# Four first-product blocks multiplied ahead of their Mish, and the seventh pair turned by DMA

## The chip, the core and the metric

The kernel runs on one core of a Trainium2 chip. The metric is the device time of one execution in microseconds, the median of several runs. The engines that appear below are PE (TensorE, matrix products and its transposes), DVE (VectorE), ACT (ScalarE), POOL (GpSimd) and SP (SyncE, which here only issues DMAs). PEld is PE's weight load. Each engine takes its own instructions in the order of the program; what has to wait, waits on semaphores.

## The reference

Attention with one extra term in the denominator, and behind it a two-layer block with Mish between the layers.

```python
# q, k, v: (8, 12, 448, 64); w_in: (768, 2048); w_out: (2048, 768)
scores = (1 / sqrt(64)) * q @ k.transpose(0, 1, 3, 2)
m = max(scores, axis=-1)
e = exp(scores - m)
attn = e / (sum(e) + exp(-m) + 1e-9)
x = (attn @ v), heads joined: (3584, 768)
h = x @ w_in                      # first product
g = h * tanh(log(1 + exp(h)))     # Mish
out = g @ w_out                   # second product
```

## The kernel before

**Pairs and units.** Two heads of one batch are a pair; a batch has six pairs, numbered through all batches (0 to 47). Three pairs are a unit, so a batch has two units. Pairs 0 to 5 (batch 0) run in a head of their own. After it comes a loop over units `u` from 2 to 17. A unit has two phases.

**Phase of the exponentials** (lines 586 to 619). It has 12 steps `n`, four for each pair. A step takes one or two score blocks of 128 rows x 448: `exps` issues the exponentials on ACT (L306), `flush_late` empties a queue of postponed copies out of PSUM onto DVE, `scores_ahead` issues the score products of the block three steps on (L272, L275, L266 and others) and their maximum on DVE (L293). There are three score tiles `sc0` to `sc2` in PSUM, of two banks each, used in turn, so the scores of step n + 3 wait for the exponentials of step n. In some steps there is other PE work: the product of a pair's weights with its values (`av_pair`, L382, whose copy into `xT` is L391), a transpose of a pair's weights on PE (`turn_on_pe`, L356, copied into `eT` by L360), and from unit 4 on pieces of the second product (L472, copied into `o_sb` by L459). In units 2 and 3 there are no such pieces.

**Phase of the first product** (lines 626 to 646). For `f` from 0 to 7 it runs `mm1_mish`: six products of 128x128 by 128x448 that make one of the 16 blocks `ff` of `h` of the batch before (L406), and Mish of it out of PSUM on ACT into `gT` (L412). Unit 2 makes the blocks 0 to 7 of batch 0, unit 3 the blocks 8 to 15. The block at f = 1 goes into a bank of `sc0`, the others take one of the two spare banks `mo`. Between the blocks stand the work for the pairs just done and for the next three: at f = 0 the denominators (L319, L323) and the division of the first pair's weights (`normalise`, seven L341 on DVE), at f = 3 that of the second pair, at f = 4 that of the third on POOL (seven L339, behind a small copy, L331); at f = 1, 3 and 5 the transposes of q and k of the next three pairs on PE (L193, into banks of `sc2` and `sc1`) and their copies out of PSUM (L214 and L227 on DVE, L235 on ACT); at f = 7 the scores of the first three steps of the next unit. At the end a one-element exponential (L649) brings ACT's table of exponentials back, since Mish has another.

**How weights are turned.** After the division a pair's weights `en` must be transposed into `eT` for `av_pair`. Most pairs go by a DMA transpose on SP's queue (L345). The pairs in `BY_PE` go by `turn_on_pe`, in four parts, at the steps listed in `TURN_AT`. `normalise` is called in an order that puts pairs of `BY_PE` last (`todo`). Pairs 6, 7 and 8 are unit 2's; 6 is the seventh pair, `HEAD` in the code. Before, 6 and 7 are both turned by PE in unit 3, and 8 by DMA.

**Other queues.** SP also issues the loads of q, k and v (L132), one pair four ahead at the steps 0, 3 and 6. POOL casts them to bf16 (L175, L176, L162) and issues the weight loads with a cast (L158, `load_w`) at the steps in `W_AT`. The blocks 8 to 11 of `h` read three pieces of `w_in` and the blocks 12 to 15 the next three. From pair 13 on, two pairs of three use a block-diagonal form of q in the tiles `q_diag`; their zero halves are written once, for pairs 13 and 14, by four DVE memsets in `evac_qk` (L223, L224), in unit 3's first-product phase.

**Banks.** `mo_take` gives the spare bank that has been free longest. In the phase of the exponentials a bank is free again when its postponed copy has run on DVE, one step later. `o_pool` has four tiles of 128 x 768 fp32, used for output rows, from unit 4 on.

Of the kernel before, what the change touches and what calls it, by code (L numbers as in the profile page):

```python
# [9 lines left out]
FP32 = mybir.dt.float32  # L10
# [9 lines left out]
def kernel(  # L20
# [91 lines left out]
    def flush_late():  # L112
        while late:
            late.popleft()()
# [86 lines left out]
    def evac_qk(p, act=False):  # L201
        if p >= N_PAIRS:
            return
        (q_ps, k_ps), own = qkT[p]
        mo_free.extend(own)
        qd = q_diag[p % 3]
        kT = qk_pool.tile([128, S], BF16, tag="kT", name="kT")
        if not is_diag(p):
            qT = qd.rearrange("d i h r -> d (i h r)")[:, 0:S]
            qkT[p] = (qT, kT)  # L210
            if act:
                nc.scalar.mul(qT, q_ps[:, 0:S], SCALE)
            else:
                nc.vector.tensor_scalar(  # L214
                    out=qT, in0=q_ps[:, 0:S], scalar1=SCALE, scalar2=None, op0=ALU.mult
                )
            if p >= DIAG_FROM:
                nc.gpsimd.tensor_copy(out=q_rest[0:64, 0, :], in_=qT[0:64, 384:S])
                nc.gpsimd.tensor_copy(out=q_rest[64:128, 1, :], in_=qT[64:128, 0:64])
        else:  # L220
            qkT[p] = (qd, kT)
            if p < DIAG_FROM + 3:
                nc.vector.memset(qd[0:64, :, 1, :], 0.0)  # L223
                nc.vector.memset(qd[64:128, :, 0, :], 0.0)  # L224
            for h in range(2):
                rows = slice(64 * h, 64 * h + 64)
                nc.vector.tensor_scalar(  # L227
                    out=qd[rows, :, h, :],
                    in0=q_ps[rows, 0:S].rearrange("d (i r) -> d i r", i=QB),
                    scalar1=SCALE, scalar2=None, op0=ALU.mult,  # L230
                )
        if p == 0 or own and not act:
            nc.vector.tensor_copy(out=kT, in_=k_ps[:, 0:S])
        else:
            nc.scalar.copy(kT, k_ps[:, 0:S])  # L235
# [160 lines left out]
        del att[p], casted[p], qkT[p]  # L396


    def mm1_mish(b, ff):
        if ff == 0:  # L400
            gT[b] = gT_pool.tile([128, FF_T, S], BF16, tag="gT", name="gT")
        flush_late()
        spare = ff % FF_U == 1
        h_ps = sc_tiles[0][:, 0, :] if spare else mo_take()
        for dm in range(DM_T):
            nc.tensor.matmul(  # L406
                h_ps[:, 0:S],
                lhsT=w_in_sb[:, dm, ff * 128 : (ff + 1) * 128],
                rhs=xT[b][:, dm, :],
                start=(dm == 0), stop=(dm == DM_T - 1),  # L410
            )
        nc.scalar.activation(out=gT[b][:, ff, :], in_=h_ps[:, 0:S], func=AF.Mish)  # L412
        if not spare:
            mo_free.append(h_ps)
# [78 lines left out]
    for g in range(B // 2):  # L493
# [12 lines left out]
        else:  # L506
# [8 lines left out]
    LAST_AV_AT = (0, 6, 9)  # L515
    HEAD = HP

    BY_PE = (2, 4, HEAD - 1, HEAD, HEAD + 1)
    TURN_AT = (
        {0: [(4, 2)], 1: [(4, 3)], **{3 + j: [(HEAD - 1, j)] for j in range(NT)}},  # L520
        {0: [(HEAD, 0), (HEAD, 1)], 1: [(HEAD, 2)], 2: [(HEAD, 3)],
         3: [(HEAD + 1, 0)], 4: [(HEAD + 1, 1)], 5: [(HEAD + 1, 2)], 6: [(HEAD + 1, 3)]},
    )
    TURN_HEAD = {
        (3, 2): [(2, 0)], (3, 3): [(2, 1)], (4, 0): [(2, 2)], (4, 1): [(2, 3)],
# [1 line left out]
    }  # L527
    AV_HEAD = {(3, 3): 0, (4, 2): 2, (4, 3): 1}
    W_HEAD = {0: 3, 1: 1, 3: 1, 4: 1}
    AV_AT = ({3: 4, 7: 3, 9: 5}, {5: 6, 8: 7, 10: 8})  # L530

    W_AT = ({5: 1, 9: 1}, {1: 1, 4: 1, 5: 1, 7: 1, 9: 1, 11: 1}, {3: 1, 5: 1, 7: 1, 9: 1})
    for which in ("qk", "v"):
# [41 lines left out]
    for u in range(UNITS_PER_B, N_UNITS + 2 * UNITS_PER_B):  # L575
# [10 lines left out]
        for n in range(steps):  # L586
# [22 lines left out]
            if u - UNITS_PER_B < len(AV_AT):  # L609
                early = AV_AT[u - UNITS_PER_B]  # L610
                if n in early:
                    av_pair(early[n])
                if u == UNITS_PER_B:
                    for part in TURN_AT[0].get(n, []):
                        turn_on_pe(*part)
            elif u == N_UNITS and n in LAST_AV_AT:
                av_pair(p0 - UNIT_PAIRS + LAST_AV_AT.index(n))
            if u - UNITS_PER_B < len(W_AT):
                load_w(W_AT[u - UNITS_PER_B].get(n, 0))
        assert done == total  # L620

        moe = u < N_UNITS + UNITS_PER_B
        b, w = (u - UNITS_PER_B) // UNITS_PER_B, u % UNITS_PER_B
        nxt = p0 + UNIT_PAIRS
        todo = sorted(range(p0, nxt), key=lambda p: p in BY_PE)
        for f in range(FF_U):
            if moe:
                mm1_mish(b, w * FF_U + f)
            if u == UNITS_PER_B and f in (2, 6):
                load_w(1)  # L630
            if not attn:
                continue
            if f == 0:
                denominators(att[p0]["whole"])
                normalise(todo[0], dma=todo[0] not in BY_PE)
            if f in (1, 3, 5):
                transpose_pair(nxt + f // 2, bank=f // 2 % 2)
                evac_qk(nxt + f // 2)
            if nxt < DIAG_FROM and f in (4, 6):
                scores_ahead(nxt * STEPS + f // 2 - 1)  # L640
            if f == FF_U - 1:
                scores_ahead(min(nxt * STEPS + 3, N_PAIRS * STEPS))
            if f == 3:
                normalise(todo[1], dma=todo[1] not in BY_PE)
            if f == 4:
                normalise(todo[2], dma=todo[2] not in BY_PE, on_pool=True)
# [37 lines left out]
```

## Time and profile before

| What | Value |
|---|---|
| median of 3 runs | 480.5 us (480.28 to 483.72) |
| profiled execution | 479.95 us |
| its span, first to last instruction | 478.0 us |
| mean granted TensorE clock | 0.982 |
| busy: PE, PEld, DVE, ACT, POOL | 443.1, 248.6, 339.1, 350.0, 181.1 us |
| mean of one L306 exponential, and of the accumulator read behind it | 637 and 206 ns |
| mean of one L293 maximum over two blocks | 968 ns |
| mean of one L406 product | 353 ns |

Times in what follows are microseconds from the span's start. A line of a timeline has start, duration, engine, line of the kernel, operation, output and input with their shapes, a count, and in brackets the idle time ahead and what ended it; merged instructions overlap in the pipe, so the distance from one start to the next (called the pitch below) is less than a duration. A line of stretches has the stretch, its length, the busy time of PE, PEld, DVE, ACT and POOL with counts, the granted clock as a share, the DMA share and the GB/s. In this execution unit 3's exponentials run from 76.75 to 91.9 and its first-product phase from there to 104.3.

### The profile page before, as it was taken

To read this page: it belongs to the slowest core of one execution; us is meant where nothing else is said; L and a number is where in the kernel's file an instruction comes from. 1 tells how busy PE (TensorE), PEld (TensorE's weight loads), DVE (VectorE), ACT (ScalarE), POOL (GpSimd) and SP (SyncE) were. 2 spreads that over 40 slices of the span, in tenths; PEclk is the share of its full clock that TensorE was granted. 3 is DMA by queue.
4 is the path that set the end of the run, shared out by engine and by line. 5 is a ranking of instruction groups with operands and counts; after the bars stand their busy time and mean duration, and the time that the engine had idled before them with its cause. 6 is when DMAs were issued, how large, how long until landed. Compare 5 with 4: busy or idle time off the path is not lost.

```text
span 478.0 us, 8924 instructions
## 1 busy us (share of the span) xinstructions
PE 443.1 (93%) x3064; PEld 248.6 (52%) x3064; DVE 339.1 (71%) x680; ACT 350.0 (73%) x919; POOL 181.1 (38%) x315
## 2 busy tenths in 40 slices
PE   4565888898999999999999999999999999999997
PEld 2233544454655555555555555556555555556565
DVE  4888987968787886878687878788787869420021
ACT  5979678878787888979787878888897978412300
POOL 4877809255514334353535242433535340300000
PEclk9998798899999999999999999999999999999999
DMA  8999969999999989899999999899989595870113
GB/s 228 220 233 220 235 100 234 162 187 238 207 217 276 206 212 219 213 203 246 193 250 182 225 167 228 211 207 234 201 233 212 156 178 127 135 164 24 43 28 105
DMA packets 202381, 90.37 MB, mean 189 GB/s; under 512 B 159072, under 2 KB 198880, under 8 KB 202336
## 3 DMA queue, kind: packets, MB, share of 16 engines
q1 hardware_dynamic: 194848, 83.51, 81.3%
q0 software_dynamic: 7488, 6.29, 8.6%
q8 instruction: 24, 0.39, 0.3%
q14 instruction: 21, 0.17, 0.1%
HBM read 45.61 MB, written 11.01 MB: 118 GB/s over the span
## 4 chain that ended last, share of the span: by engine, by line
PE 76%; ACT 10%; DVE 9%; issue 2%; DMA 1%; POOL 0%; SPq 0%; DVEq 0%; ACTq 0%; POOLq 0%
PE mo L472 26%; PE mo L406 25%; ACT en L306 9%; PE sc L382 6%; DVE negm L293 6%; PE sc L266 5%; PE sc L406 4%; PE sc L193 3%; PE sc L272 2%; PE mo L356 1%; PE mo L382 1%; DVE en L341 1%; PE sc L280 1%; DVE eT L360 1%; DMA k_f<-in_k_dram 1%
## 5 line engine op out<-in xcount | busy, mean ns | idle before, releaser
L306 ACT ACTIVATE en<-sc,negm 128x448 bf16<-128x448 f32 x336 | 209.6, 637 | 26.4 <-DVE xT L391 10.4
L293 DVE TENSOR_REDUCE negm<-sc 128x2 f32<-128x896 f32 x192 | 180.7, 968 | 55.8 <-PE sc L275 26.0
L472 PE MATMUL mo<-w_out_sb,gT 128*128 128x384 bf16 (+1 forms) x912 | 142.3, 301 | 0.0
L406 PE MATMUL mo<-xT,w_in_sb 128*128 128x448 bf16 x672 | 137.7, 353 | 0.6 <-DVE xT L391 0.6
L412 ACT ACTIVATE gT<-mo 128x448 bf16<-128x448 f32 x112 | 61.3, 547 | 68.2 <-PE mo L406 68.1
L472 PEld LDWEIGHTS <-gT 128*128 128x128 bf16 x912 | 84.1, 98 | 48.2 <-issue 5.7
L339 POOL TENSOR_SCALAR en<-en,rden 128x448 bf16<-128x448 bf16 x122 | 76.4, 646 | 80.7 <-DVE rden L331 76.9
L406 PEld LDWEIGHTS <-w_in_sb 128*128 128x128 bf16 x768 | 72.9, 98 | 64.0 <-issue 3.0
L306 ACT ACTIVATION_READ_ACCUMULATOR en<-sc,negm 128x1 f32 x336 | 69.3, 206 | 0.0
L175 POOL CAST q_bf<-q_f 112x512 bf16<-112x512 f32 x47 | 29.0, 617 | 98.4 <-DMA q_f<-in_q_dram 98.0
L341 DVE TENSOR_SCALAR en<-en,rden 128x448 bf16<-128x448 bf16 x214 | 58.6, 345 | 0.9
L459 DVE COPY o_sb<-mo 128x384 f32<-128x384 f32 (+1 forms) x65 | 32.2, 495 | 35.1 <-PE mo L472 34.8
L266 PE MATMUL sc<-kT,qd 128*128 128x448 bf16 x168 | 47.7, 354 | 0.3 <-ACT en L306 0.2
L272 PE MATMUL sc<-kT,qd 64*128 64x448 bf16 x72 | 25.1, 411 | 12.7 <-ACT en L306 11.1
L382 PE MATMUL sc<-eT,v_bf 112*64 112x448 bf16 x288 | 34.1, 357 | 1.9 <-ACT en L306 1.7
L162 POOL CAST v_bf<-v_f 112x512 bf16<-112x512 f32 x48 | 29.5, 616 | 9.7 <-DMA v_f<-in_v_dram 8.8
L382 PEld LDWEIGHTS <-v_bf 112*64 112x64 bf16 x384 | 21.0, 112 | 22.8 <-issue 13.6
L176 POOL CAST k_bf<-k_f 112x512 bf16<-112x512 f32 x47 | 28.9, 616 | 7.5 <-DMA k_f<-in_k_dram 7.0
L227 DVE TENSOR_SCALAR qd<-sc 64x448 bf16<-64x448 bf16 x48 | 18.7, 389 | 11.9 <-PE sc L193 11.2
L266 PEld LDWEIGHTS <-qd 128*128 128x128 bf16 x168 | 16.3, 97 | 18.0 <-issue 9.2
L275 PE MATMUL sc<-kT,qd 64*128 64x448 bf16 x72 | 25.4, 415 | 0.0
L472 PE MATMUL mo<-w_out_sb,mid 128*128 128x384 bf16 x128 | 24.9, 326 | 0.0
(57 smaller groups left out, 340.1 us busy)
## 6 DMA issues: line engine op xcount, KB each, us to landing
q_f<-in_q_dram SPq DMA_DIRECT2D x48, 224.0 KB, 5.1
k_f<-in_k_dram SPq DMA_DIRECT2D x48, 224.0 KB, 5.4
v_f<-in_v_dram SPq DMA_DIRECT2D x48, 224.0 KB, 5.7
w_in_sb<-in_moe_w_in_dram POOLq DMA_DIRECT2D x12, 256.0 KB, 6.1
w_out_sb<-in_moe_w_out_dram POOLq DMA_DIRECT2D x8, 384.0 KB, 7.6
out_dram<-o_sb SPq DMA_DIRECT2D x7, 336.0 KB, 3.3
out_dram<-o_sb SPq DMA_DIRECT2D x8, 288.0 KB, 4.6
out_dram<-o_sb SPq DMA_DIRECT2D x8, 240.0 KB, 2.9
```

Of the source, the lines that this page charges most:

```text
L162: nc.gpsimd.tensor_copy(out=casted[p][2], in_=loaded.pop(p)[2])
L266: nc.tensor.matmul(sc[:, bk, 0:S], lhsT=qT[:, i].rearrange("d h r -> d (h r)"), rhs=kT, start=True, stop=True,)
L272: nc.tensor.matmul(sc[:, 0, 0:S], lhsT=qT[0:64, qa : qa + 128], rhs=kA, start=True, stop=True)
L293: nc.vector.tensor_reduce(out=negm, in_=sc[:, 0 : len(cols), 0:S], axis=AX.X, op=ALU.max, negate=True)
L306: nc.scalar.activation(out=st["en"][:, :, c, 0:SP_], in_=sc[:, bk, 0:S].rearrange("q (j c) -> q j c", j=NT), func=AF.Exp, bias=st["negm"][ ...
L339: nc.gpsimd.tensor_scalar(scalar2=1.0, op0=ALU.mult, op1=ALU.mult, **args)
L341: nc.vector.tensor_scalar(scalar2=None, op0=ALU.mult, **args)
L382: nc.tensor.matmul(av[h * 64 : (h + 1) * 64, 0:S], lhsT=v_bf[:, h, j * D : (j + 1) * D], rhs=e_h, start=(j == 0), stop=(j == NT - 1),)
L406: nc.tensor.matmul(h_ps[:, 0:S], lhsT=w_in_sb[:, dm, ff * 128 : (ff + 1) * 128], rhs=xT[b][:, dm, :], start=(dm == 0), stop=(dm == DM_T - 1),)
L412: nc.scalar.activation(out=gT[b][:, ff, :], in_=h_ps[:, 0:S], func=AF.Mish)
L459: nc.vector.tensor_copy(out=o_sb[:, cols], in_=st["o"][:, 0:n_cols])
L472: nc.tensor.matmul(st["o"][:, 0:n_cols], lhsT=src[:, ff, c0 : c0 + 128], rhs=w_out_sb[:, ff, cols], start=(ff == 0), stop=(ff == FF_T - 1),)
```

## The change

- In unit 3's phase of exponentials, at the steps 5, 7, 9 and 10, `mm1_ahead` issues the products of the blocks 8, 9, 10 and 11 of batch 0 into an `mo` bank, and queues a DVE copy into an fp32 tile of `o_pool` (128 x 448 used), which runs at the next step.
- In unit 3's first-product phase the order of the blocks is 8, 12, 9, 13, 10, 14, 11, 15. The blocks 8 to 11 have only their Mish there, read from the fp32 tile. The bank of `sc0` goes to the block at f = 1, which is now 12.
- Pair 6 leaves `BY_PE`: it is turned by DMA. So `todo` in unit 2 is 6, 8, 7 in place of 8, 6, 7: pair 6 is divided and sent at f = 0, pair 8 at f = 3.
- Pair 7 is turned by PE at the steps 1 to 4 of unit 3 (before 3 to 6; pair 6 was at 0 to 2). The value products of pairs 6, 7 and 8 stand at the steps 3, 6 and 8 (before 5, 8 and 10).
- The zero halves of `q_diag[1]` and `q_diag[2]` are written by four POOL memsets at the end of unit 3's exponentials.

```diff
             qkT[p] = (qd, kT)
-            if p < DIAG_FROM + 3:
-                nc.vector.memset(qd[0:64, :, 1, :], 0.0)
-                nc.vector.memset(qd[64:128, :, 0, :], 0.0)
...
-    def mm1_mish(b, ff):
-        if ff == 0:
-            gT[b] = gT_pool.tile([128, FF_T, S], BF16, tag="gT", name="gT")
-        flush_late()
-        spare = ff % FF_U == 1
-        h_ps = sc_tiles[0][:, 0, :] if spare else mo_take()
+    def mm1(b, ff, h_ps):
         for dm in range(DM_T):
...
+    h_sbs = {}
+
+    def mm1_ahead(b, ff):
+
+        h_ps = mo_take()
+        mm1(b, ff, h_ps)
+        h_sb = o_pool.tile([128, d_model], FP32, tag="o_sb", name="o_sb")
+        h_sbs[b, ff] = h_sb
+
+        def evac():
+            nc.vector.tensor_copy(out=h_sb[:, 0:S], in_=h_ps[:, 0:S])
+            mo_free.append(h_ps)
+
+        late.append(evac)
+
+    def mm1_mish(b, ff, spare):
+        if ff == 0:
+            gT[b] = gT_pool.tile([128, FF_T, S], BF16, tag="gT", name="gT")
+        flush_late()
+        if (b, ff) in h_sbs:
+            nc.scalar.activation(out=gT[b][:, ff, :], in_=h_sbs.pop((b, ff))[:, 0:S], func=AF.Mish)
+            return
+        h_ps = sc_tiles[0][:, 0, :] if spare else mo_take()
+        mm1(b, ff, h_ps)
         nc.scalar.activation(out=gT[b][:, ff, :], in_=h_ps[:, 0:S], func=AF.Mish)
...
-    BY_PE = (2, 4, HEAD - 1, HEAD, HEAD + 1)
+    BY_PE = (2, 4, HEAD - 1, HEAD + 1)
     TURN_AT = (
         {0: [(4, 2)], 1: [(4, 3)], **{3 + j: [(HEAD - 1, j)] for j in range(NT)}},
-        {0: [(HEAD, 0), (HEAD, 1)], 1: [(HEAD, 2)], 2: [(HEAD, 3)],
-         3: [(HEAD + 1, 0)], 4: [(HEAD + 1, 1)], 5: [(HEAD + 1, 2)], 6: [(HEAD + 1, 3)]},
+        {1 + j: [(HEAD + 1, j)] for j in range(NT)},
     )
...
-    AV_AT = ({3: 4, 7: 3, 9: 5}, {5: 6, 8: 7, 10: 8})
+    AV_AT = ({3: 4, 7: 3, 9: 5}, {3: 6, 6: 7, 8: 8})
+    FIRST_AT = {5: FF_U, 7: FF_U + 1, 9: FF_U + 2, 10: FF_U + 3}
+    SECOND = [ff for i in range(4) for ff in (FF_U + i, FF_U + 4 + i)]
...
                 if n in early:
                     av_pair(early[n])
+                if u == UNITS_PER_B + 1 and n in FIRST_AT:
+                    mm1_ahead(0, FIRST_AT[n])
...
+        if u == UNITS_PER_B + 1:
+            for t_ in q_diag[1:]:
+                nc.gpsimd.memset(t_[0:64, :, 1, :], 0.0)
+                nc.gpsimd.memset(t_[64:128, :, 0, :], 0.0)
+
...
             if moe:
-                mm1_mish(b, w * FF_U + f)
+                mm1_mish(b, SECOND[f] if u == UNITS_PER_B + 1 else w * FF_U + f, spare=f == 1)
```

## The prediction

> **What bounds the kernel now.** I began with the page's chain of waits, to see which engine sets the end.
>
> ```profile
> PE 76%; ACT 10%; DVE 9%; issue 2%; DMA 1%; POOL 0%; SPq 0%; DVEq 0%; ACTq 0%; POOLq 0%
> ```
>
> Three quarters of the chain are PE, so PE work that is taken off a stretch where PE is the limit, and put where PE idles, is worth its length. The change lies in unit 3, so next came the busy time by stretch: unit 3's exponentials, its first-product phase, then the same two of unit 4.
>
> ```profile
> 76.75:91.90 15.15, 11.62 (x86) 6.71 (x86) 12.97 (x19) 13.44 (x43) 9.94 (x16) 0.79 1.16 208
> 91.90:104.30 12.40, 12.40 (x87) 6.75 (x86) 8.98 (x29) 8.60 (x18) 4.65 (x9) 0.98 0.90 160
> 104.30:119.30 15.00, 13.07 (x89) 7.22 (x88) 12.76 (x18) 13.56 (x44) 7.83 (x14) 1.00 1.08 228
> 119.30:130.10 10.80, 10.80 (x87) 6.48 (x86) 7.63 (x24) 8.18 (x16) 5.00 (x10) 1.00 1.31 205
> ```
>
> In unit 3's first-product phase PE is busy for all of 12.40 us, DVE and ACT for under 9. In the exponentials PE leaves 3.5 us, and runs at a mean clock of 0.79. The chain in order of time shows PE's part:
>
> ```profile
> 88.64 2.84 PE mo L382 x16
> 91.48 1.67 PE mo L406 x6
> 93.16 1.13 PE sc L406 x6
> ...
> 100.02 2.29 PE mo L406 x12
> ...
> 102.89 1.28 ACT L649
> ```
>
> Two value products and the first block ran at a low clock (one value product is 0.95 at full clock, one block 1.13). Then ACT and DVE in the same place, and ACT's pitch in unit 4's phase:
>
> ```profile
> 92.17 1.28 ACT L412 ACT_TABLE_LOAD   x1
> ...
> 121.18 0.54 ACT L412 ACTIVATE gT<-sc 128x448 bf16<-128x448 f32 x1
> 121.60 0.54 ACT L235 COPY kT<-sc 128x448 bf16<-128x448 bf16 x1
> 122.01 0.57 ACT L412 ACTIVATE gT<-mo 128x448 bf16<-128x448 f32 x1
> ```
> ```profile
> 87.74 2.61 DVE L293 TENSOR_REDUCE negm<-sc 128x2 f32<-128x896 f32 x3
> 90.26 0.61 DVE L391 CAST xT<-mo 128x448 bf16<-128x448 f32 x1
> 91.52 0.62 DVE L391 CAST xT<-mo 128x448 bf16<-128x448 f32 x1 [0.65 <-PE mo L382]
> 92.18 0.18 DVE L319 SCALAR_TENSOR_TENSOR den<-sums,expm 128x21 f32<-128x21 f32 x1
> 92.40 0.29 DVE L323 RECIPROCAL rden<-den 128x21 f32<-128x21 f32 x1
> 92.73 1.81 DVE L341 TENSOR_SCALAR en<-en,rden 128x448 bf16<-128x448 bf16 x7
> ```
>
> ACT issues a Mish or copy each 0.42 us when nothing holds it, and DVE begins the division as soon as its last copy is done. Last SP's queue, the landing of its transposes between 60 and 160, and the first consumer in unit 4:
>
> ```profile
> 67.42 4.20 SPq L345 DMA_TRANSPOSE eT<-en  x1
> 71.72 0.53 SPq L132 DMA_DIRECT2D q_f<-in_q_dram  x1
> ...
> 95.03 13.69 SPq L345 DMA_TRANSPOSE eT<-en  x3
> ```
> ```profile
> DMA to landing us min/median/max: 6.1/6.6/9.3
> ```
> ```profile
> 105.67 0.95 PE L382 MATMUL sc<-eT,v_bf 112*64 112x448 bf16 x8 [0.32 <-ACT en L306]
> ```
>
> **Unit 2: the transposes.** Pair 6 goes at 67.42 in pair 8's place; it lands by 75 to 77 and is read at step 3, near 82.5. Pair 8 follows at 71.7 and lands by 81 at the latest; it is read near 88.5. Behind it on SP the nine loads of pairs 13 to 15 start 4.2 us later, at 75.9. They land 4.2 to 7.0 us after issue in this stretch, so POOL's casts of pairs 13 and 14 slip by 2 to 3 us, and so does the weight load queued behind the first of them (at 81.33 before), of the last piece that block 12 needs. With 6.1 to 7.7 us to landing it is there by 90 to 92; block 12 is due at 92.5 (below). q and k of these pairs are due from 94. All covered, by a margin under 2 us for the weight piece; if that is gone, PE waits for what is missing.
>
> **Unit 3: the exponentials.** PE loses four turns at 0.55 and gains four blocks at 1.13: 2.3 us more, against 3.5 idle. DVE loses four L360 copies and gains four fp32 copies, 128x448. L391, the same input shape, has a pitch of 0.53, and so has L360: no change in sum, only in place. Up to the maximum of step 8 (ends 86.67) as many copies lie ahead as before. From there: copy of block 8 (0.53), maximum of step 9 (1.0), L391 of pair 7 (0.53), maximum of 10 (1.0), copy of block 9 (0.53), maximum of 11 (0.53). Step 9's maximum is ready at 88.2 (before 88.74), step 11's at 90.8. ACT starts step 9 at 88.3, step 10 at 89.8, and ends at 91.85 with L316, 0.3 earlier than before. The moved blocks stand ahead of the next scores on PE; with 1.13 + 0.3 a step on PE and 1.53 on DVE, DVE still sets the step.
>
> The last block is the tight one. Its bank is that of pair 8's value product, whose copy stands behind the maximum of step 11: 90.8 + 0.53 = 91.3. So block 11 runs from 91.35 to 92.5, and its copy, which DVE must take before the denominators, ends at 93.05. L319 then starts 0.87 later than the 92.18 shown.
>
> **Unit 3: the first-product phase, engine by engine.** PE: block 12 to 93.65, then 3 transposes of 0.4 and blocks 13 to 15, ended at 98.3 with its waits; before 102.3. ACT: table 1.28 to 93.15, eleven instructions of about 0.43 with waits for blocks 13, 14 and 15 (1.0 in all), to 98.8, table and L649 (1.4): exponentials at 100.3. Mish from fp32 in SBUF is in no row. Bounds: 0.54, as from PSUM, and 0.617, a cast of 112x512 from SBUF on ACT in the head; 4 x 0.07 = 0.3 at most, inside the waits. I take 0.54, the nearer shape. DVE: from 93.05, in the pitches of before, denominators 0.55, seven L341 1.80, L214 0.37, two L227 0.82, seven L341 1.73, L331 0.15, two L227 0.80: 99.3. The four memsets (0.24 each, 1.3 with their gaps) are gone; on POOL they fall between its last weight issue and 93, where it sits idle for 8 us. First maximum 1.03: 100.3. So ACT and DVE meet at 100.35, against 104.29: **3.95 us gained.**
>
> **Unit 4.** Pair 9's division ends at 95.4; SP took 0.57 to start and 6.2 to land: 102.1. Its value product came 1.38 behind the first exponential, so would now be due at 101.7: 0.4 lost, on the way to the scores and maximum of step 3, which DVE and ACT then wait for. The next two transposes follow SP's own pace (4.3 each): landed at 106.4 and 110.8, due at 107.5 and 112.4. SP's loads start at 108.8, as before, while what reads them is due 3.5 us earlier: pair 17's casts end near 118, its transposes are due at 121.8; the last second-product weights land 8.2 us after 118.3 to 119, due from 127.5. All hold, by 1 to 4 us. Behind unit 4 nothing is changed, and units repeat at PE's pace, so the shift lasts. **Net 3.95 - 0.4 = 3.55 us.** The profiled execution of 479.95 (span 478.0 and 1.95 around it) becomes 476.4; it lay 0.55 under the median of the runs, which becomes 477.0.
>
> **Rivals.**
> - *No late division.* If the bank waits overlap better, ACT is the floor: 93.15 + 11 x 0.42 + 1.4 = 99.2, or 5 us gained, and the median 475.5. For it: all waits are sums of pitches that I made by hand. Against: DVE's order, which is fixed. 0.16.
> - *Given back in unit 4.* The transpose of pair 9 takes the 9.3 seen at the longest, not 6.2: 3.1 lost, 480.0. For it: that row, and that SP and its loads don't move with the rest. Against: 9.3 belongs to the stretch with a DMA share of 1.31, and here it was 0.57 from 92 to 96. 0.12.
> - *Half clock (slower).* These are single microseconds of before, with the clock third from the end:
>
> ```profile
> 79.00:80.00 1.00, 0.88 (x7) 0.39 (x6) 0.86 (x2) 1.00 (x5) 1.00 (x2) 0.50 0.96 252
> 87.00:88.00 1.00, 0.00 (x0) 0.00 (x0) 1.00 (x3) 1.00 (x3) 0.00 (x0) 1.00 1.32 196
> 90.00:91.00 1.00, 1.00 (x8) 0.37 (x4) 0.88 (x2) 1.00 (x5) 0.00 (x0) 0.50 1.33 206
> ```
>
>   The clock is 0.50 from 79 to 82 and 89 to 92, each time behind a gap on PE. If it stays at 0.50 from 82 to the end of the exponentials, four blocks cost 2.26 each (+4.5), two value products 2.84 (+0.95), four scores +0.2 each: 6.3 us, nearly all on PE's path to block 11, since PE has 7.8 us of work in the 8.1 from 84.4. Then 477.0 + 6.3 = 483.3; with blocks 12 and 13 as well, 485.6. It ends slower than before once more than 3.55 of the 6.3 comes, over half of the stretch. For it: in the head the clock stayed at 0.50 from about 44.5 to 54.8, with PE busy nine tenths from 46 on. Against: steps 1 to 3 are as before, so the clock should rise at 82 again, and the gap at 87 is filled by a block. 0.10.
>
> The Trainium skill, page "TensorE: Matmul & The Clock Gate", section "Part 1: The HAM clock gate", has half clock after an idle window of about 3.4 us and full clock after as long a busy one; by it the fuller stretch stays at full clock and this rival falls away. The trace agrees on the length of the low stretches here, but a gap of only 1.4 us (86.9 to 88.3) was enough to bring one, and the head's low stretch lasted three times as long, so I leave the rival its chance.
>
> **The numbers.** My forecast, 3.55 us with about a microsecond of hand-summed waits either way (2.2 to 4.6 gained, 475.9 to 478.3), has 0.62. Within 1% (475.7 to 485.3) is what a measurement of this kernel can't tell from no change. Faster beyond that: the first rival, 0.16. Slower beyond: the half clock that lasts into the next phase or a missing weight piece, 0.07. Within: 0.77. The range reaches from 475.2, past the ACT floor, to 481.0, past the transpose that takes 9.3; about 0.2 is left out, mostly the half clock.
>
> **What would show it.** Right: exponentials of unit 4 near 100.3, L319 of unit 3 near 93, block 11 ended past 92, a clock of 1.0 from 82 on, pair 9's value product waiting some tenths for its DMA, and all of unit 5 3.5 us earlier. Wrong: maxima of unit 3 late behind blocks at 2 us each; block 12 waiting for its weights; a wait of over 1 us at a value product of unit 4; POOL's casts of pairs 16 and 17 holding unit 4's transposes.

## The result and the profile after

| | before | after |
|---|---|---|
| median of 20 runs each, us | 480.14 (478.97 to 483.72) | 483.63 (481.1 to 486.95) |
| ratio after / before, with its 95% interval | | 1.0062 [1.0045, 1.0079] |
| profiled execution, us | 479.95 | 484.43 |
| its span, us | 478.0 | 482.4 |
| mean granted TensorE clock | 0.982 | 0.985 |

The changed kernel is 0.6% slower, 3.5 us by the medians, where I had forecast 3.5 us less. The ratios leave out the runs in a slower state (one of e6 below, two of e10, three of e12), and the medians take in all runs.

Line numbers below are those of the changed kernel where its trace is read: exponentials L303, maximum L290, denominators L316 and L320, division L338, DMA transpose L342, value product L379, first product L398, copy into SBUF L415, Mish from SBUF L425 and from PSUM L429, second product L489, table of exponentials L674.

The shares of the chain of waits by engine, after:

```profile
PE 70%; ACT 12%; DVE 9%; DMA 5%; issue 3%; POOL 1%; SPq 0%; DVEq 0%; ACTq 0%
```

DMA has grown from 1% to 5% of the chain, 19 us or so longer in it, and PE has given up 6%. Almost all of that is two transposes that unit 5 waits for (10.69 and 7.69). The chain only runs through them: 19 us more of it don't cost 19 us, but waits for transfers are where to look. To place the loss I used ACT's table loads as marks, since each phase begins with one. After, on ACT's timeline:

```profile
68.67 1.28 ACT L429 ACT_TABLE_LOAD   x1
...
95.60 1.28 ACT L425 ACT_TABLE_LOAD   x1
...
103.59 1.28 ACT L674 ACT_TABLE_LOAD   x1
...
121.24 1.28 ACT L429 ACT_TABLE_LOAD   x1
...
131.88 1.28 ACT L674 ACT_TABLE_LOAD   x1
...
149.93 1.28 ACT L429 ACT_TABLE_LOAD   x1
```

The same marks before stand at 64.99, 92.17, 102.89, 119.44, 128.76 and 145.53. The first belongs to unit 2, ahead of anything that the change touches, and is already 3.68 late. Taken off, the rest reads as a shift, negative where the changed kernel is ahead: **-0.25** at the end of unit 3's exponentials, **-2.98** at the end of its first-product phase, **-1.88** and **-0.56** at the same two places of unit 4, **+0.72** at the end of unit 5's exponentials. From unit 6 on both kernels keep the same pace but for one step of 0.10 us, and 0.72 is what is left at the end of the span. So the trace holds three stories: the head (3.68), a gain of 2.98 up to the end of unit 3, and 3.70 given back in the units 4 and 5.

The stretches of the changed kernel between these marks (a phase of exponentials is counted from 1.40 behind its L674 mark, where the first exponential can start), first unit 3's two phases, then unit 4's, then unit 5's exponentials:

```profile
80.41:95.60 15.19, 12.97 (x91) 6.67 (x91) 12.83 (x19) 13.89 (x45) 11.36 (x19) 0.89 1.11 236
95.60:104.99 9.39, 8.50 (x65) 4.69 (x64) 8.24 (x26) 8.26 (x14) 2.98 (x8) 1.00 1.31 172
104.99:121.24 16.25, 13.65 (x93) 7.49 (x91) 12.81 (x18) 13.68 (x45) 7.05 (x12) 1.00 1.10 237
121.24:133.28 12.04, 10.88 (x87) 6.49 (x86) 9.52 (x24) 8.21 (x14) 8.44 (x15) 1.00 1.27 203
133.28:149.93 16.65, 15.41 (x99) 8.09 (x97) 12.54 (x18) 13.85 (x45) 3.72 (x7) 1.00 1.07 234
```

Unit 3's first-product phase went from 12.12 (92.17 to 104.29) to 9.39, and PE is no longer busy throughout. Unit 4's two phases took 16.25 and 12.04, against 15.15 and 10.73 before, and unit 5's exponentials 16.65 against 15.36, with the same work in them. DVE's busy time in unit 4's first-product phase rose from 7.70 to 9.52 for the same 24 instructions.

**Where it is given back.** Three places. The first is the value product of pair 9 in unit 4, on PE's timeline after:

```profile
107.46 0.95 PE L379 MATMUL sc<-eT,v_bf 112*64 112x448 bf16 x8 [0.96 <-DMA eT<-en]
```

Its transpose was issued at 99.49 and took 7.8 us to land. The second is the division of pair 12 at the start of unit 4's first-product phase, DVE before and then DVE after:

```profile
120.00 1.81 DVE L341 TENSOR_SCALAR en<-en,rden 128x448 bf16<-128x448 bf16 x7
```
```profile
121.86 3.58 DVE L338 TENSOR_SCALAR en<-en,rden 128x448 bf16<-128x448 bf16 x7
```

The same seven instructions take twice as long. POOL's timeline shows what runs beside them after, and where the same casts of pair 17 stood before:

```profile
121.85 0.64 POOL L175 CAST q_bf<-q_f 112x512 bf16<-112x512 f32 x1
122.40 0.70 POOL L176 CAST k_bf<-k_f 112x512 bf16<-112x512 f32 x1
123.06 0.60 POOL L162 CAST v_bf<-v_f 112x512 bf16<-112x512 f32 x1
123.61 1.49 POOL L158 DMA_DIRECT2D w_out_sb<-in_moe_w_out_dram  x2
```
```profile
116.62 0.63 POOL L175 CAST q_bf<-q_f 112x512 bf16<-112x512 f32 x1
117.18 0.63 POOL L176 CAST k_bf<-k_f 112x512 bf16<-112x512 f32 x1
117.74 0.62 POOL L162 CAST v_bf<-v_f 112x512 bf16<-112x512 f32 x1
```

Before, the casts were done ahead of the division. Now, counted from the head, DVE arrives 1.8 us earlier (121.86 less 3.68, against 120.00) and POOL 1.6 later (121.85 less 3.68, against 116.62). The third place is the chain in order of time, which follows the late division into unit 5:

```profile
122.56 2.88 DVE en L338 x6
125.44 0.06 DVE qd L214
125.50 10.69 DMA eT<-en
```

The transpose of pair 12 is issued at 125.50, beside the weight loads just shown, lands after 10.69 us, and the value product of unit 5 waits for it. PE's timeline there, after and before:

```profile
125.79 0.36 PE L193 MATMUL sc<-ident,q_bf 112*128 112x112 bf16 x4 [1.16 <-DVE qd L214]
...
131.89 3.44 PE L489 MATMUL mo<-w_out_sb,gT 128*128 128x192 bf16 x28
136.33 0.95 PE L379 MATMUL sc<-eT,v_bf 112*64 112x448 bf16 x8 [1.00 <-DMA eT<-en]
```
```profile
128.77 3.44 PE L472 MATMUL mo<-w_out_sb,gT 128*128 128x192 bf16 x28
132.15 0.95 PE L382 MATMUL sc<-eT,v_bf 112*64 112x448 bf16 x8
```

Before, that product ran without a gap. But its transpose, issued at 121.87, had taken 9.3 us, by its line's transposes from 121 to 123 in the trace before:

```profile
DMA to landing us min/median/max: 9.3/9.3/9.3
```

It landed at 131.2, 1.0 us ahead of its use. In this pair of traces, that margin is what was used up.

### The profile page after: what moved, and what is told of

It reads as the page before. It is cut to its first block, busy times and chain, and to the rows that moved or that the text cites. A ratio compares the mean times of both kernels' runs of the same rounds, so it can differ in the third digit from the quotient of the medians.

```text
span 482.4 us, 8867 instructions
## 1 busy us (share of the span) xinstructions
PE 440.6 (91%) x3036; PEld 245.9 (51%) x3036; DVE 345.1 (72%) x676; ACT 350.0 (73%) x919; POOL 182.5 (38%) x319
## 4 chain that ended last, share of the span: by engine, by line
PE 70%; ACT 12%; DVE 9%; DMA 5%; issue 3%; POOL 1%; SPq 0%; DVEq 0%; ACTq 0%
PE mo L489 25%; PE mo L398 23%; ACT en L303 9%; PE sc L379 6%; PE sc L263 5%; DVE negm L290 5%; DMA eT<-en 4%; PE sc L193 3%; PE sc L398 3%; PE sc L269 2%; DVE en L338 2%; PE mo L379 1%; DMA w_in_sb<-in_moe_w_in_dram 1%; PE mo L353 1%; DMA k_f<-in_k_dram 1%
## 5 line engine op out<-in xcount | busy, mean ns | idle before, releaser
L303 ACT ACTIVATE en<-sc,negm 128x448 bf16<-128x448 f32 x336 | 209.2, 636 | 32.0 <-DVE negm L290 14.9
L290 DVE TENSOR_REDUCE negm<-sc 128x2 f32<-128x896 f32 x192 | 180.7, 969 | 57.2 <-PE sc L272 24.8
L489 PE MATMUL mo<-w_out_sb,gT 128*128 128x384 bf16 (+1 forms) x912 | 142.3, 301 | 0.0
L398 PE MATMUL mo<-xT,w_in_sb 128*128 128x448 bf16 x672 | 137.6, 352 | 1.3 <-DMA w_in_sb<-in_moe_w_in_dram 0.6
L489 PEld LDWEIGHTS <-gT 128*128 128x128 bf16 x912 | 84.1, 98 | 48.0 <-issue 5.5
L429 ACT ACTIVATE gT<-mo 128x448 bf16<-128x448 f32 x108 | 59.1, 547 | 65.1 <-PE mo L398 64.7
L398 PEld LDWEIGHTS <-w_in_sb 128*128 128x128 bf16 x768 | 72.8, 98 | 64.0 <-issue 3.2
L303 ACT ACTIVATION_READ_ACCUMULATOR en<-sc,negm 128x1 f32 x336 | 69.1, 206 | 0.0
L338 DVE TENSOR_SCALAR en<-en,rden 128x448 bf16<-128x448 bf16 x214 | 65.1, 375 | 0.9
L379 PE MATMUL sc<-eT,v_bf 112*64 112x448 bf16 x288 | 34.1, 357 | 3.8 <-DMA eT<-en 2.2
L269 PE MATMUL sc<-kT,qd 64*128 64x448 bf16 x72 | 25.5, 411 | 12.8 <-ACT en L303 11.1
L379 PEld LDWEIGHTS <-v_bf 112*64 112x64 bf16 x384 | 20.3, 110 | 24.1 <-issue 13.3
L489 PE MATMUL mo<-w_out_sb,mid 128*128 128x384 bf16 x128 | 24.9, 326 | 0.0
```

The source lines that it names most:

```text
L269: nc.tensor.matmul(sc[:, 0, 0:S], lhsT=qT[0:64, qa : qa + 128], rhs=kA, start=True, stop=True)
L290: nc.vector.tensor_reduce(out=negm, in_=sc[:, 0 : len(cols), 0:S], axis=AX.X, op=ALU.max, negate=True)
L303: nc.scalar.activation(out=st["en"][:, :, c, 0:SP_], in_=sc[:, bk, 0:S].rearrange("q (j c) -> q j c", j=NT), func=AF.Exp, bias=st["negm"][ ...
L338: nc.vector.tensor_scalar(scalar2=None, op0=ALU.mult, **args)
L379: nc.tensor.matmul(av[h * 64 : (h + 1) * 64, 0:S], lhsT=v_bf[:, h, j * D : (j + 1) * D], rhs=e_h, start=(j == 0), stop=(j == NT - 1),)
L398: nc.tensor.matmul(h_ps[:, 0:S], lhsT=w_in_sb[:, dm, ff * 128 : (ff + 1) * 128], rhs=xT[b][:, dm, :], start=(dm == 0), stop=(dm == DM_T - 1),)
```

## The experiments

In all of them the shift is counted as above, from the first mark. The table gives each run's median, its ratio to the kernel before measured beside it, and the shift of its profiled execution at the ends of unit 3, unit 4 and unit 5, each time behind the unit's first-product phase.

| run | median, us | ratio [95%] | unit 3 | unit 4 | unit 5 |
|---|---|---|---|---|---|
| after, first trace | 483.63 | 1.0062 [1.0045, 1.0079] | -2.98 | -0.56 | +0.61 |
| e1_after_again | 483.35 | 1.0055 [1.0036, 1.0073] | -2.79 | -1.26 | +1.38 |
| e2_after_spread | 484.97 | 1.0095 [1.0065, 1.0124] | -1.89 | -0.11 | +1.28 |
| e3_before_spread | 482.98 | 1.0050 [1.0026, 1.0073] | -1.13 | -1.13 | -1.31 |
| e4_turn_only | 483.78 | 1.0080 [1.0053, 1.0108] | -0.79 | +0.05 | +1.13 |
| e5_before_again | 480.57 | 1.0007 [0.9987, 1.0027] | -0.90 | -0.90 | +0.21 |
| e6_blocks_only | 483.96 | 1.0075 [1.0052, 1.0099] | -1.44 | +0.11 | +2.44 |
| e7_turn_only | 482.60 | 1.0046 [1.0021, 1.0070] | -2.09 | -0.41 | +1.18 |
| e8_loads_first | 481.80 | 1.0025 [1.0002, 1.0049] | -2.97 | +0.97 | +0.23 |
| e9_weights_early | 481.59 | 1.0015 [0.9993, 1.0037] | -2.19 | +2.97 | +2.23 |
| e10_after_both | 489.09 | 1.0198 [1.0151, 1.0244] | -2.17 | +3.40 | +2.66 |
| e11_before_both | 483.61 | 1.0065 [1.0040, 1.0090] | -0.90 | +1.76 | +1.02 |
| e12_turn_both | 492.84 | 1.0185 [1.0137, 1.0232] | +3.41 | +6.07 | +5.33 |
| e13_split | 484.80 | 1.0085 [1.0048, 1.0123] | -2.98 | +2.26 | +1.53 |
| e14_after_half | 478.88 | 0.9963 [0.9937, 0.9990] | -2.71 | -2.45 | -3.19 |
| e15_loads_half | 478.20 | 0.9944 [0.9922, 0.9965] | -2.19 | -1.83 | -2.56 |
| e16_before_half | 479.28 | 0.9976 [0.9955, 0.9997] | -1.12 | -1.11 | -1.85 |
| e17_gated | 478.00 | 0.9954 [0.9939, 0.9968] | -2.98 | -2.45 | -3.19 |
| e18_behind | 478.11 | 0.9957 [0.9941, 0.9973] | -2.64 | -2.26 | -3.00 |

### Is the head's 3.68 us the change's?

The head's instructions are the same in both kernels. Yet in the first trace after, three early divisions on DVE took 5.20 us where before they took 0.82. DVE's timeline after, then before:

```profile
17.40 5.20 DVE L338 TENSOR_SCALAR en<-en,rden 128x448 bf16<-128x448 bf16 x3
```
```profile
17.36 0.82 DVE L341 TENSOR_SCALAR en<-en,rden 128x448 bf16<-128x448 bf16 x3
```

POOL was at work without a gap beside the long ones: it issued three weight loads, divided four blocks and cast until 22.46. In none of the other traces did the three take over 1.50. e1 is the changed kernel unaltered.

> The changed kernel, unaltered. In its first profile the head alone, whose program is the same on every engine as before, came out 3.7 us longer: three divisions on DVE (L338, at 17.4) lasted 5.2 us in place of 0.8 while POOL went from issuing weight loads straight into its own divisions and casts. Theory A (chance of an execution, set by when the first loads land): the times fall into two groups about 3.5 us apart, near 481.5 and 484.5, and a profile shows either 5.2 or 0.8. Theory B (the change lengthens the head every time): one group near 484, and 5.2 in the profile.

Its first mark stands at 65.56, so most of the 3.68 was this one execution; but its units 4 and 5 gave back 4.2 us again. Of the three places, the first is missing: pair 9's transpose landed after 7.0, and PE did not wait for it. The other two are there: the division of pair 12 took 3.48, its transpose 12.0, and the value product of unit 5 waited 2.32. e2, e3 and e4 spread the weight loads of the head, on the kernel after, the kernel before, and the kernel before with pair 6 turned by DMA:

```diff
-    W_HEAD = {0: 3, 1: 1, 3: 1, 4: 1}
+    W_HEAD = {0: 1, 1: 1, 2: 1, 3: 1, 4: 1, 5: 1}
```

> The changed kernel with the head's first three weight loads issued one per pair instead of three at once, so that POOL is done with them before DVE's first divisions at 17.4. Theory A: the three divisions take 0.8 to 1.2, unit 2's first Mish table load begins near 65 as before the change, and the time is one group near 481 (480.1 plus the 0.7 that the units 3 to 5 lost net in the profile). Theory B: still near 484.

> The kernel before with the same spreading of the head's weight loads. Theory A: the same 480 as before, since it met the stretch of 5.2 in few runs; e2 minus e3 is then what units 3 to 5 do, 0.7 to 1.5 us lost. If spreading itself costs or brings something, it shows here.

> Of the change only pair 6 turned by DMA, with the later order of pairs and value products, on the kernel before with spread weight loads; no block is multiplied ahead. Theory C (SP's queue gives the gain back: the second transpose in unit 2 pushes nine loads and two weight loads 4 us later, and they then run beside unit 3's transposes): pair 9's transpose lands later than the 6.2 of before, POOL's casts of pair 13 wait for their loads, and the time is 0.5 to 3 us above e3. Theory D (what was lost in units 4 and 5 comes from their being due earlier, not from the extra transpose): same as e3 within 0.5, or faster by the DVE copies saved.

A miss: spreading costs by itself. e3 is 0.5% over the kernel before, its first mark at 68.83, e2's at 68.62 and e4's at 67.47. So against the kernel before the medians of these three tell nothing on the change. Against e3, which has the same spreading, e2 is 2.0 us longer and e4 0.8, with intervals that overlap. Their shifts show unit 4 and 5 losing 3.2 us in e2 and 1.9 in e4, and nothing in e3. e5 is the kernel before, unaltered.

> The kernel before, unaltered, sent like an experiment: a second profile of it and a second set of times. If the head's length is a matter of chance for each execution of this program, its times lie on the 480.2 of the runs of before, and the head ends (unit 2's first Mish table load) within 0.5 of 65.0 in the profile. If sending a kernel as an experiment alone adds time, it comes out near 483 like the last four.

The first mark lies at 66.83 this time, and the median did not move. Over the three traces that run before's program up to this mark (64.99, e5 66.83, e16 65.64) it has a mean of 65.8; in e1, which has the change, it is 65.56. The head varies from one execution to the next, and no run ties that to the change.

e5 shows a second thing. On its PE timeline, at the end of unit 3's exponentials, stand the value products and the first block that the chain of before has at 88.64 and 91.48 with 2.84 and 1.67 us:

```profile
90.44 1.70 PE L382 MATMUL mo<-eT,v_bf 112*64 112x448 bf16 x16
92.80 1.30 PE L406 MATMUL mo<-xT,w_in_sb 128*128 128x448 bf16 x6 [0.66 <-DVE xT L391]
```

The low clock of this place in the trace that I predicted from did not come again. e5 is 0.90 ahead of that trace behind unit 3, and e3, e11 and e16 are 0.9 to 1.1 ahead as well. So the first trace was about 1.0 us worse up to the end of unit 3 than the other four of the kernel before and its variants, and of the gain of 2.98 about 2.0 is the change's.

e5 shows a third thing. The kernel before can lose in unit 5 too. There pair 12's transpose took 10.4, and PE's timeline has

```profile
133.34 0.95 PE L382 MATMUL sc<-eT,v_bf 112*64 112x448 bf16 x8 [0.19 <-DMA eT<-en]
```

The next pair's transpose, held back on SP's queue, landed at 139.1, and PE stood 0.98 ahead of its value product. Unit 5's exponentials came out 1.2 us longer than in the first trace (from -0.90 to +0.31). So the margin of 1.0 us is not there in every execution, even without the change.

### Which part gives the time back?

e6 has the blocks ahead, but pair 6 is turned by PE and the value products stand as before. e7 has the turn by DMA alone, with no blocks ahead. e6's edit, against the kernel after (the turns on PE stand at their old steps too):

```diff
-    BY_PE = (2, 4, HEAD - 1, HEAD + 1)
+    BY_PE = (2, 4, HEAD - 1, HEAD, HEAD + 1)
-    AV_AT = ({3: 4, 7: 3, 9: 5}, {3: 6, 6: 7, 8: 8})
+    AV_AT = ({3: 4, 7: 3, 9: 5}, {5: 6, 8: 7, 10: 8})
```

> The changed kernel with pair 6 turned by PE again and the order of pairs and value products of before; the four blocks still go ahead. Theory C (SP's queue gives the gain back): SP's loads start near 71.7 again, so units 3 to 5 keep most of the gain, and from the end of the head to the end of the span it is 1.5 to 3.5 us shorter than before (413.0 before, 413.7 and 414.3 in two profiles of the change). Theory D (what is due earlier waits for SP and POOL anyway): no shorter than before, 413 or more, with value products of units 4 and 5 waiting for DMA.

> The kernel before with pair 6 turned by DMA, the order of pairs and value products as in the change, no block ahead. Theory C: 1 to 3 us longer than before from the end of the head on (414 to 416), with unit 3's first transpose landing late and units 4 and 5 waiting for it. Theory D: equal to before within 0.5.

One suspicion was the transpose added to SP's queue. As the main cause it falls: e6 has no added transpose and gives back most, 3.9 us. e7 is 2.09 ahead at the end of unit 3 and gives back 3.3. In both the division of pair 12 is long (3.61 and 3.51) and the transpose behind it lands after 11.1. What the two have in common is that unit 4 starts earlier. Only the first place may hang on the added transpose: pair 9's landed after 6.4 in e6 and nothing waited for it, and after 9.6 in e7, where PE waited 0.58.

The other two places come with the change each time. In the six traces that have the blocks, the turn or both and unit 4's loads where they were (after, e1, e2, e4, e6, e7), the division of pair 12 took 2.59 to 3.70, its transpose landed after 10.7 to 12.0, and the value product of unit 5 waited 1.0 to 2.3. In the three of the kernel before with all its weight loads (before, e3, e5) it is 1.81, then 9.1 to 10.4, and a wait of 0.19 at most.

At the end of unit 3 the turn alone (e7) is 2.09 ahead, the blocks alone (e6) 1.44, both together 2.98, and the kernel before about 1.0 in its other traces. These are single traces, and e4, the turn alone on spread loads, is only 0.79 ahead, so how the gain divides between blocks and turn is not shown.

### Is it the late supply of unit 4?

The remaining theory: SP's loads of the pairs 16 to 18 and POOL's casts and weight loads don't come forward with the rest, because SP's queue is held by three transposes in order (14.54 us from 99.49), and what comes earlier now meets them. e8 puts the loads of 13 to 15 and 16 to 18 ahead of the transposes; e9 moves four weight loads from unit 4 to unit 2, so that all are issued by the end of unit 3; e10 does both, e11 and e12 do both on the kernel before and on the turn alone, and e13 has e8's loads with two of the weight loads moved to unit 2. The edits of e8 and e9:

```diff
+            if n in LOAD_AT and u not in (UNITS_PER_B + 1, UNITS_PER_B + 2):
+                load_pair(p0 + LOAD_AT.index(n) + LEAD)
+            if n >= steps - 3 and u in (UNITS_PER_B, UNITS_PER_B + 1):
+                load_pair(p0 + UNIT_PAIRS + LEAD + n - (steps - 3))
             if n in LOAD_AT:
-                load_pair(p0 + LOAD_AT.index(n) + LEAD)
...
-    W_AT = ({5: 1, 9: 1}, {1: 1, 4: 1, 5: 1, 7: 1, 9: 1, 11: 1}, {3: 1, 5: 1, 7: 1, 9: 1})
+    W_AT = ({5: 1, 9: 1, 10: 2, 11: 2}, {1: 1, 4: 1, 5: 1, 7: 1, 9: 1, 11: 1})
```

> The changed kernel with the loads of pairs 13 to 15 issued in the last three steps of unit 2's exponentials, where the DMA engines idle, and those of 16 to 18 in the last three of unit 3's, ahead of the transposes instead of behind them. Theory C: casts in units 3 and 4 wait for no load, unit 3's first transpose lands in 6 to 6.5 again, and most of the 3 to 4 us lost in units 4 and 5 stays: 410 to 411.5 from the end of the head to the end of the span, 2 to 3 us under the change. Theory D: no better than the change, since loads beside the transposes slow them as much.

> The changed kernel with the last four w_out loads of unit 4 moved out of it: four more weight loads are issued in the last two steps of unit 2's exponentials, where the DMA engines idle, and the rest shift up. Theory E (the gain is given back where unit 4's DMA supply, whose place in time SP's queue fixes, meets work that is due earlier: POOL's casts of pair 17 run beside DVE's division of pair 12, 3.5 in place of 1.8, and pair 12's transpose lands in 10.7 to 12 in place of 9.3 beside loads and weight loads): the transpose of pair 12 lands in 7 to 9, the division still takes 3.5 since SP's loads are where they were; 412 to 413.3 from the end of the head to the end of the span (413.7 and 414.3 in the change). Theory F (PE's and ACT's own work loses it): unchanged at 414.

> The changed kernel with the earlier loads of e8 and the earlier weight loads of e9. Theory E: neither the long division nor a transpose of over 8 us to landing in units 3 to 5, the 3.0 gained at the end of unit 3 stay: 410 to 410.7 from the end of the head to the end of the span, and 477.5 us. Theory F: 413 or more.

> The kernel before with the same two moves of loads. Before, units 4 and 5 ran at the pace of all later units, so Theory E has nothing to win there: 413 from the end of the head to the end of the span, 480. If it is 1 us or more faster, the moves are worth something by themselves, and e10 has to be read against this one.

> Pair 6 by DMA alone (e7, which had gained 2.1 at the end of unit 3 and gave 3.3 back) with the same two moves of loads. Theory E: the 2.1 stay, 411 from the end of the head to the end of the span, and the four blocks are worth the 0.9 between this and e10.

> The changed kernel with the earlier loads of e8, two weight loads moved from unit 4 to the end of unit 2, and the two that remain in unit 4 issued behind its casts. By what was seen (a transpose beside or shortly behind weight loads and loads lands in 9 to 15.5, a clear one in 6 to 6.5) pairs 9, 11 and 12 should land in 7 to 8; 410.5 to 411.5 from the end of the head to the end of the span and 478 us. If the loads only run into another transpose, it is 413 or more.

None of them kept the gain of unit 3 to the end, though e8 and e9 come nearer to before than the changed kernel does. e10 and e12 are the worst of all, 2.0% and 1.9% over the kernel before, where 477.5 us was expected of e10; their traces are of the fastest of their runs and show less than the medians lose. Wherever weight loads came to stand in these six, they met another transpose. In e9 it was pair 9's. Its chain in order of time, and the issue of weights on POOL just ahead of it:

```profile
96.76 10.08 DMA eT<-en
```
```profile
90.86 2.22 POOL L158 DMA_DIRECT2D w_out_sb<-in_moe_w_out_dram  x3
```

That cost e9 5.2 us in unit 4's exponentials, while its pair 12, with no weights left in unit 4, landed after 6.2. In e8 the two weight loads at 108.59 met pair 11's transpose (issued 106.8, landed after 9.6); PE stood 2.40 us, and the next block took 2.45 us for its six products in place of 1.30. In e13 transposes took 11.2, 10.1 and 9.8, in e11 up to 15.5, in e12 15.4. The losses differ with what was met, and the kernel before loses as well (e11, 2.7 us in unit 4), so this is no property of the blocks alone.

e14 to e16 take the weight loads of unit 4 away instead of moving them: half of the second product's weights are never loaded, and the product reads the other half twice. e14 is the kernel after, e15 e8, e16 the kernel before.

```diff
-        for h in range(2):
+        for h in range(1):
...
-                    rhs=w_out_sb[:, ff, cols],
+                    rhs=w_out_sb[:, ff, half],
```

> The changed kernel without the last four w_out loads, the second product reading the first half of w_out's columns for the second half too. Theory E: pair 12's transpose lands in 6 to 8 in place of 10.7 to 12 and its value product waits for no DMA; the division of pair 12 beside POOL's casts stays at 3.5 and costs 1.3 in unit 4's first-product phase; 411.5 to 412.8 from the end of the head to the end of the span. Theory F (own work of PE, DVE and ACT): 414.

> The same, without the last four w_out loads, on e8, whose loads stand ahead of the transposes. Theory E: no long division and no late transpose in units 3 to 5, and the 3.0 gained in unit 3 stay whole: 410.0 to 410.5 from the end of the head to the end of the span. Theory F: 413.

> The kernel before without the last four w_out loads. Theory E: pair 12's transpose lands in 6 to 7 in place of 9.3, but nobody waited for it, so 413.0 to 413.3 from the end of the head to the end of the span, as before. If it is shorter by 1 or more, the four loads cost the kernel before too, and e14 and e15 must be read against that.

e14 keeps its gain: -2.71 behind unit 3, -2.52 at the end of unit 5's exponentials, where the kernel after has +0.72. Its pair 12, by its line's transposes from 120 to 124 and by PE's timeline (the second product is L490 there):

```profile
L342 SPq DMA_TRANSPOSE eT<-en x1: 4174/4174/4174, 121.2 to 121.2; - x1
...
DMA to landing us min/median/max: 6.2/6.2/6.2
```
```profile
127.61 3.44 PE L490 MATMUL mo<-w_out_sb,gT 128*128 128x192 bf16 x28
130.98 0.95 PE L379 MATMUL sc<-eT,v_bf 112*64 112x448 bf16 x8
```

6.2 instead of 10.7, SP held for 4.2 instead of 8.6, and no gap on PE.

The trace of the control e16 stays where it was behind unit 3 (-1.12, then -1.19). But its median is 479.28 against 480.54 for the kernel before measured beside it, ratio 0.9976 [0.9955, 0.9997], and its trace has 411.3 from the first mark to the end of the span, where the first trace has 413.0. That is the case named in its expectation: the four loads cost the kernel before as well, 1.3 us by the medians. By the ratios they cost it 0.2% and the changed kernel 1.0% (1.0062 against 0.9963), so the larger share comes with the change. Read against e16, e14 and e15 are 0.4 and 1.1 us faster, with intervals that overlap its own. Without these loads the change is no longer slower; that it is faster, these medians don't show.

The traces also grade the division of pair 12: 3.58 in the kernel after, beside three casts without a gap and the weight issues behind them, 2.52 in e14, beside two whole casts with gaps of 0.3 between them, 1.81 in e15 with POOL idle. The Trainium skill, page "SBUF — State Buffer", section "SBUF: two separate sides", has one pair of ports that GpSimd shares with those DVE instructions that work through two ports, and whichever starts first has it for its whole instruction. The trace agrees in kind, since the seven instructions of 0.25 us lost 1.8 in sum beside a busy POOL. That the division is such an instruction, no run here shows.

### A version that keeps it

e17 is the kernel after with e8's loads and with the four weight loads of unit 4 together, behind a small POOL copy that waits for a value product's output, so that they start when the unit's transposes have nearly all landed (112.85, the last at 113.2). e18 is the same without that copy.

```diff
-    W_AT = ({5: 1, 9: 1}, {1: 1, 4: 1, 5: 1, 7: 1, 9: 1, 11: 1}, {3: 1, 5: 1, 7: 1, 9: 1})
+    W_AT = ({5: 1, 9: 1}, {1: 1, 4: 1, 5: 1, 7: 1, 9: 1, 11: 1}, {7: 4})
...
+            if u == UNITS_PER_B + 2 and n == 7:
+                nc.gpsimd.tensor_copy(out=gate, in_=xT[1][:, 4, 0:64])
```

> The changed kernel with the earlier loads of e8, and the last four w_out loads issued together behind POOL's casts of pair 17 and a small POOL copy that waits for unit 4's value product of pair 10, so that they start when pair 11's transpose has nearly landed. By the collisions seen, pair 11 lands in 6.5 to 7.5 and pair 12 in 8 to 10, due about 10 after its issue: 410.5 to 411.8 from the end of the head to the end of the span, 478 to 479 us. If pair 12 takes the 11 to 12 of e1, its value product waits 1 to 2 and it is 413.

> The same without the small copy: the four loads go as soon as the casts of pair 17 are done, some 1.5 earlier, beside more of pair 11's transpose and less of pair 12's. Pair 11 lands in 7.5 to 9.6, pair 12 in 7 to 9; 411 to 413 from the end of the head to the end of the span. If both transposes are hurt, it is worse than e8's 413.3.

e17's POOL, DVE and PE in unit 4 and at the start of unit 5 (its lines are one higher):

```profile
112.61 0.24 POOL L643 COPY gate<-xT 128x64 bf16<-128x64 bf16 x1 [2.16 <-DVE xT L389]
112.85 3.04 POOL L159 DMA_DIRECT2D w_out_sb<-in_moe_w_out_dram  x4
```
```profile
118.98 1.81 DVE L339 TENSOR_SCALAR en<-en,rden 128x448 bf16<-128x448 bf16 x7
```
```profile
131.13 0.95 PE L380 MATMUL sc<-eT,v_bf 112*64 112x448 bf16 x8
```

Division and value product are as before the change, and the five transposes from 97 to 126 land in 6.1 to 7.3 us. Of -2.98 behind unit 3, -2.52 is left at the end of unit 5's exponentials. The median is 478.0 against 480.0 for the kernel before measured beside it, ratio 0.9954 [0.9939, 0.9968]: the blocks, the turn by DMA and the two moves of the supply together are worth 2.0 us. e18 has the same within the intervals, so the position of the loads suffices and the waiting copy is not needed. No run makes these two moves on the kernel before, which by e16 has 1.3 us to win at its weight loads; so how much of the 2.0 needs the blocks and the turn is not shown.

## Why the prediction was wrong

- **The gain in unit 3: right in kind, a quarter too large.** 3.95 was forecast and 2.98 came. The exponentials ended 0.25 earlier, against 0.3 forecast; no weight piece was late (block 12, at 96.33, follows block 11 at once); POOL's four memsets took 0.51 at most and ended by 96.3, hidden; Mish from SBUF took 0.58, inside the waits. PE and DVE in this phase:

```profile
94.06 2.43 PE L398 MATMUL mo<-xT,w_in_sb 128*128 128x448 bf16 x12 [0.46 <-DVE o_sb L415]
96.33 1.30 PE L398 MATMUL sc<-xT,w_in_sb 128*128 128x448 bf16 x6
...
99.77 0.36 PE L193 MATMUL sc<-ident,q_bf 112*128 112x112 bf16 x4 [0.61 <-DVE qd L214]
```
```profile
96.53 0.62 DVE L415 COPY o_sb<-mo 128x448 f32<-128x448 f32 x1 [0.51 <-PE mo L398]
97.07 0.17 DVE L316 SCALAR_TENSOR_TENSOR den<-sums,expm 128x21 f32<-128x21 f32 x1
```

  Less the head's 3.68, the denominators start at 93.39 (forecast 93.05): the tight place was the last block's copy, as said. The rest of the shortfall is the 0.61 that pair 13's transposes waited for a DVE copy behind the division; my sum of DVE had that copy in its place, but PE's had no wait for it.
- **The baseline.** The 12.4 of the first-product phase began with a block at a low clock, behind two value products at the same, and e5 has neither. I had seen them and put their removal into the gain; about 1.0 of the 2.98 comes in the kernel before as well when the low clock stays away.
- **The step that failed is "Unit 4".** "Its value product came 1.38 behind the first exponential, so would now be due at 101.7: 0.4 lost": the wait was 0.96, since the transpose took 7.8 and not 6.2, and the phase came out 1.1 longer (in e1 there was no wait, and 0.25 longer). "All hold, by 1 to 4 us": it asked whether POOL's casts end ahead of the transposes that need them, which they did, and not what they run beside. The casts of pair 17 met the division (1.81 became 3.58), 1.3 lost in this phase. The rows of before had this in them: the division at 120.00, moved 3.5 forward, starts at 116.5, and the casts ran from 116.62 to 118.36. "Behind unit 4 nothing is changed, and units repeat at PE's pace, so the shift lasts": pair 12's transpose, beside the same phase's weight loads, landed after 10.7, and unit 5 lost another 1.3. It was my own row: the 9.3 at the longest in the landing times was this transpose, 1.0 us ahead of its use before. What the runs showed in place of a shift that lasts: with the loads where they were, all six traces lose 1.9 to 4.2 us between the ends of unit 3 and unit 5; with them moved (e17, e18) none is lost.
- **Rivals.** "Given back in unit 4" had the cause, a transpose that takes 9.3 or more, but put it on pair 9 and priced it at 3.1 once. It is three smaller losses, 3.7 in sum, with the longest wait for a transpose in unit 5 (1.00, and 2.32 in e1). "Half clock" did not come: the clock was full from 86 on, and none of the four blocks took over 1.31. "No late division" did not come either; ACT still waited 0.67 for the transposes.
- **Range and sign.** The range reached to one late transpose, 481.0. There were two, and a division with them, and the median of 483.63 lies past it; as a ratio it is inside the 1% that I held for not to be told from no change, but its interval of 0.2% either way does tell it.
- **What stays open.** The profiled executions end 0.7 (after) and 1.3 (e1) behind before, counted from the head, but the medians are 3.1 to 3.5 apart. The traces of the kernel before differ among themselves, too: e5 ends 0.3 behind the first and e3 1.2 ahead of it. Collisions that differ from execution to execution fit that, e6 with +2.44 among them, and so would a head that is late more often; single traces don't divide the two. Open too is what e17's two moves would bring without the blocks and the turn, and how the gain of unit 3 divides between these two.

## What to carry to other kernels

When a stage is made shorter, list what feeds the next two stages from queues that don't come forward with it, and ask of each transfer not only whether it lands in time but what it now runs beside. The longest landing time in a queue is a consumer's margin waiting to be used up: find which transfer it is and when its reader is due. Take the stretch to be improved from two traces where there are two, for the gain hangs on how that stretch happened to run.

## What the hardware showed that I had not expected

- A DMA transpose of a pair's weights landed after 6.1 to 6.2 us and held SP for 4.2 to 4.3 in the kernel before (the three issued from 95.0 to 104.5). Beside weight loads issued by POOL, and SP's own loads, it took up to 15.5 and held SP for 11.2 (e11, issued at 68.4); in the kernel after pair 12's took 10.7 and held SP for 8.6. Landing late alone is no sign of weight loads: with all of them done, one issued at 149.1 before took 8.5 and held SP for 4.6.
- Beside back-to-back POOL instructions a DVE division took twice as long (1.81 to 3.58). In one head three of its instructions took 5.20 instead of 0.82, again beside a busy POOL; that POOL was the cause there is not shown.
- The same head program took between 65.0 and 66.8 us to its end in the traces of the kernel before, a spread of 1.8 us.
